# Last output tile in column parts of 384 and 128, the last 128 columns stored by two queues of 64 token rows each

## The chip, the cores and the metric

The kernel runs on one core of one Trainium2 chip. The metric is the device time of one execution, in microseconds (us). I quote medians over several executions. The trace's own span, from the first to the last recorded instruction, is about 1.7 us shorter than that time (178.7 against 180.4 us in the profiled run of the kernel before). PE is the tensor engine, ACT the scalar engine and DVE the vector engine; SP only issues transfers here. A transfer (DMA) is issued on the queue of SP or ACT, its packets then move the bytes, and I say that it has landed when the last of its 16 landing records is in.

## The reference

Two branches read the same 2048 tokens of 512 values, and a gate mixes them:

```python
x = A_x
g = sigmoid((x * gate_w).sum(-1, keepdims=True))
a = linear_attention(x, A_wqkv) @ A_wo        # 32 heads of 16
b = (silu(x @ B_w1) * (x @ B_w3)) @ B_w2      # F = 1376
return g * a + (1 - g) * b                    # 1 x 2048 x 512, bfloat16
```

## The kernel before

Tokens go through in four blocks of 512, each with four output tiles of 128 token rows. An output tile sums, in one PSUM tile, 4 matmuls of the attention branch, 1 of the FFN remainder and 10 of the FFN. It is then scaled per token and stored. Only the sixteenth tile, with which the kernel ends, is cut by columns:

```python
# loads, all on the SP queue
w2_r = B_w2[0:FM, :].rearrange("(fc f) d -> f fc d", f=P)
for fcs in (slice(0, FC // 2), slice(FC // 2, FC)):
    dq.dma_start(out=w2_sb[:, fcs, :], in_=w2_r[:, fcs, :])
# ... (cut)
def emit_out(tb, tt):
    # ... (cut)
    if t < NT - 1:
        parts = [(0, D, True)]
    else:
        h, q3 = D // 2, 3 * D // 4
        parts = [(0, h, True), (h, q3, False), (q3, D, True)]
    o_out = work.tile([P, D], BF16, tag="o_out", name="o_out")
    lo = 0
    for i, (a, b, store) in enumerate(parts):
        o_ps = psX.tile([P, b - a], FP32, tag=f"XP{2 + (tt + i) % 2}", name="o_ps")
        # ... 4 + 1 + 10 matmuls of b - a columns into o_ps (cut)
        if i < 2:
            nc.scalar.activation(out=o_out[:, a:b], in_=o_ps[:], func=ACT.Copy,
                                 scale=omg[:, t : t + 1])
        else:
            nc.vector.tensor_scalar(out=o_out[:, a:b], in0=o_ps[:],
                                    scalar1=omg[:, t : t + 1], scalar2=None, op0=ALU.mult)
        if store:
            rows = out_pairs[t // 2, t % 2] if t < TPB else out2d[t * P : (t + 1) * P, :]
            nc.sync.dma_start(out=rows[:, lo:b], in_=o_out[:, lo:b])
            lo = b
```

Of the kernel before, what the change touches and what calls it, by code (L numbers as in the profile page):

```python
# [9 lines left out]
ALU = mybir.AluOpType  # L10
# [7 lines left out]
def kernel(  # L18
# [12 lines left out]
    nc = tc.nc  # L31
    P = nc.NUM_PARTITIONS

    Bb, S, D = A_x.shape
# [4 lines left out]
    NT = S // P  # L39
    TB = 512  # L40
    NTB = S // TB
    TPB = TB // P
    FC = F // P
    FR = F - FC * P
    FM = FC * P
# [4 lines left out]
    out2d = out.flatten_outer_dims()  # L50
# [21 lines left out]
    w2_sb = consts.tile([P, FC, D], BF16, name="w2_sb")  # L72
# [7 lines left out]
    dq = nc.sync  # L80
    x_pairs = x2d[0:TB, :].rearrange("(g p j) d -> g p j d", p=P, j=2)
    out_pairs = out2d[0:TB, :].rearrange("(g p j) d -> g j p d", p=P, j=2)
# [6 lines left out]
    for tb in range(1, NTB):  # L89
        dq.dma_start(  # L90
            out=xT[:, :, tb * TB : (tb + 1) * TB], in_=x2d[tb * TB : (tb + 1) * TB, :],
# [3 lines left out]
            out=x_sb[:, tb * TPB : (tb + 1) * TPB, :], in_=x_r[:, tb * TPB : (tb + 1) * TPB, :]  # L95
# [4 lines left out]
    with nc.allow_non_contiguous_dma(reason="one gate weight per partition and chunk"):  # L100
        dq.dma_start(
            out=wr_sb[:, :, 2 * FR : NR], in_=gate_w.rearrange("(kc d o) -> d kc o", d=P, o=1)
# [3 lines left out]
        dq.dma_start(out=w1_sb[:, :, fsl], in_=w1_r[:, :, fsl])  # L106
        dq.dma_start(out=w3_sb[:, :, fsl], in_=w3_r[:, :, fsl])
    dq.dma_start(out=wo_sb[:], in_=A_wo.rearrange("(kc d) n -> d kc n", d=P))
    w2_r = B_w2[0:FM, :].rearrange("(fc f) d -> f fc d", f=P)
    for fcs in (slice(0, FC // 2), slice(FC // 2, FC)):  # L110
        dq.dma_start(out=w2_sb[:, fcs, :], in_=w2_r[:, fcs, :])
    dq.dma_start(out=w2r_sb[:FR, :], in_=B_w2[FM:F, :])

    pk_sb = consts.tile([P, NT, D], BF16, name="pk_sb")
# [5 lines left out]
        out=bm, in_=bm, pattern=[[-Dh, HPC], [0, Dh]], compare_op=ALU.is_ge, fill=0.0,  # L120
# [3 lines left out]
        out=bm, in_=bm, pattern=[[Dh, HPC], [0, Dh]], compare_op=ALU.is_ge, fill=0.0,  # L124
# [6 lines left out]
    omg = consts.tile([P, NT], FP32, name="omg")  # L131
# [200 lines left out]
    def emit_out(tb, tt):  # L332
        t = tb * TPB + tt
        tsl = slice(tt * P, (tt + 1) * P)

        if t < NT - 1:
            parts = [(0, D, True)]
        else:
            h, q3 = D // 2, 3 * D // 4
            parts = [(0, h, True), (h, q3, False), (q3, D, True)]  # L340
        o_out = work.tile([P, D], BF16, tag="o_out", name="o_out")
        lo = 0
        for i, (a, b, store) in enumerate(parts):
            o_ps = psX.tile([P, b - a], FP32, tag=f"XP{2 + (tt + i) % 2}", name="o_ps")
            for c in range(KC):
                nc.tensor.matmul(  # L346
                    o_ps[:], lhsT=st[tb, "pqT"][:, c, tsl], rhs=W_sb[:, c, a:b],
                    start=(c == 0), stop=False,
                )
            nc.tensor.matmul(  # L350
                o_ps[:], lhsT=st[tb, "hTr"][:FR, tsl], rhs=w2r_sb[:FR, a:b],
                start=False, stop=False,
            )
            for fc in range(FC):
                nc.tensor.matmul(  # L355
                    o_ps[:], lhsT=st[tb, "hT"][:, fc, tsl], rhs=w2_sb[:, fc, a:b],
                    start=False, stop=(fc == FC - 1),
                )
            if i < 2:
                nc.scalar.activation(  # L360
                    out=o_out[:, a:b], in_=o_ps[:], func=ACT.Copy, scale=omg[:, t : t + 1]
                )
            else:
                nc.vector.tensor_scalar(  # L364
                    out=o_out[:, a:b], in0=o_ps[:], scalar1=omg[:, t : t + 1], scalar2=None,
                    op0=ALU.mult,
                )
            if store:
                rows = out_pairs[t // 2, t % 2] if t < TPB else out2d[t * P : (t + 1) * P, :]
                nc.sync.dma_start(out=rows[:, lo:b], in_=o_out[:, lo:b])  # L370
                lo = b


    k0 = [psM.tile([P, D], FP32, tag="mm", name=f"k0_{t}") for t in range(TPB)]
# [33 lines left out]
    for c in range(KC):  # L408
# [7 lines left out]
        out=kvT_sb[:], in0=kvT_ps[:],  # L416
# [26 lines left out]
    for tb in range(NTB):  # L443
        for fc in range(FC if tb == 0 else 0, FC):
            emit_ffn(tb, fc)
        nx = tb + 1
        for tt in range(TPB):
            if nx < NTB:
                emit_q(nx, tt, psX, "XP0")
                if tt % 2 == 0:  # L450
                    emit_rem(nx, tt // 2, psX, "XP1")
            emit_out(tb, tt)
            if nx < NTB:
                emit_den(nx, tt)
        if nx < NTB:
            emit_norm(nx)
# [30 lines left out]
```

## Time and profile before

| what | kernel before |
|---|---|
| time, median of 6 executions | 180.28 us (180.18 to 180.48) |
| span of the profiled one | 178.7 us |
| tensor engine (PE) busy | 174.1 us, 97% |
| last tile on PE | 172.46 to 175.80 us |
| last scaling (DVE) | 175.88 to 176.23 us |
| last store issued | 176.30 us |

The page's first lines give each engine's busy time with its share and its number of instructions. The second part gives the clock granted to PE in tenths, over 40 slices:

```profile
span 178.7 us, 2472 instructions
...
PE 174.1 (97%) x877; PEld 84.6 (47%) x893; DVE 119.3 (67%) x205; ACT 66.6 (37%) x126; POOL 61.3 (34%) x69
...
PEclk9999999999999999999999999999999999999999
```

PE has work nearly all the time, at full clock. So the change can act only where PE's work ends and the last result has still to leave the chip. The chain that ended last, in the view from 169 us on (start, duration, what):

```profile
...
172.46 0.44 PE o_ps L346 x4
172.90 0.11 PE o_ps L350
173.01 1.09 PE o_ps L355 x10
174.10 0.22 PE o_ps L346 x4
174.33 0.06 PE o_ps L350
174.38 0.56 PE o_ps L355 x10
174.94 0.22 PE o_ps L346 x4
175.17 0.06 PE o_ps L350
175.23 0.57 PE o_ps L355 x10
...
175.88 0.35 DVE o_out L364
```

The three groups of 15 matmuls take 1.64, 0.84 and 0.85 us. What follows is in the timeline from 175.7 us on, and in the DMA issues from 176.3 us on (operation, KB, us from issue to landing):

```profile
176.30 0.33 SPq L370 DMA_DIRECT2D out_dram<-o_out  x1
```

```profile
out_dram<-o_out SPq DMA_DIRECT2D x1, 64.0 KB, 1.5
```

The issue keeps the SP queue busy for 0.33 us, and the data has landed 1.5 us after the issue began. The records of the single packets and landings are finer. Counted from the end of the last scaling, the first packet leaves at 0.90 us, the last landing is at 1.60 us, and the span ends at 2.45 us. I call that last figure the tail.

### The profile page before, as it was taken

The numbers are of one execution on the slowest core, as the hardware profiler recorded it, in microseconds if no ns is written. First come the engines' busy times: TensorE is split into PE (matmuls) and PEld (weight loads), VectorE is DVE, ScalarE is ACT, GpSimd is POOL, SyncE is SP. The second block draws the span as 40 slices with busy tenths as digits, with TensorE's granted clock in tenths as the row PEclk, the third lists the DMA queues.
The fourth block names the chain that finished last, engine by engine and source line by source line (L and its number), as shares of the span: only waits on it lengthen the run. The fifth ranks groups of instructions, "written<-read, shape, count | busy, mean of one in ns | idle before, by whom it ended". The sixth has DMA issues, their size and how long they took to land.

```text
span 178.7 us, 2472 instructions
## 1 busy us (share of the span) xinstructions
PE 174.1 (97%) x877; PEld 84.6 (47%) x893; DVE 119.3 (67%) x205; ACT 66.6 (37%) x126; POOL 61.3 (34%) x69
## 2 busy tenths in 40 slices
PE   8999999999999999999999999999999999999993
PEld 4444444474444545444454544444545444444463
DVE  1588867997998837398786375978754669776000
ACT  3642323476533333342433333342433323341221
POOL 5187575736353323262003232620032328100000
PEclk9999999999999999999999999999999999999999
DMA  5999999901005010124000111240001023300011
GB/s 178 263 272 245 267 321 369 321 6 28 9 12 107 0 48 29 44 55 92 0 4 6 38 37 37 59 93 2 0 7 59 14 62 64 61 0 0 29 44 50
DMA packets 29085, 14.88 MB, mean 83 GB/s; under 512 B 19632, under 2 KB 28816, under 8 KB 29072
## 3 DMA queue, kind: packets, MB, share of 16 engines
q1 hardware_dynamic: 28800, 14.46, 30.2%
q10 hardware_dynamic: 272, 0.26, 0.5%
q8 instruction: 7, 0.11, 0.3%
q14 instruction: 6, 0.05, 0.1%
HBM read 8.42 MB, written 2.10 MB: 59 GB/s over the span
## 4 chain that ended last, share of the span: by engine, by line
PE 97%; issue 1%; DVE 0%; DVEq 0%
PE o_ps L355 19%; PE gate_ps L310 19%; PE up_ps L318 19%; PE o_ps L346 8%; PE q_ps L217 8%; PE XP L204 8%; PE k_ps L184 6%; PE r_ps L241 3%; PE k L184 2%; PE o_ps L350 2%; PE warm L161 2%; PE xTp L174 1%; PE kvT_ps L411 1%; PE W_ps L438 0%; DVE o_out L364 0%
## 5 line engine op out<-in xcount | busy, mean ns | idle before, releaser
L310 PE MATMUL gate_ps<-xT,w_sb 128*128 128x512 bf16 x156 | 40.7, 379 | 0.2
L318 PE MATMUL up_ps<-xT,w_sb 128*128 128x512 bf16 x156 | 40.5, 379 | 0.2
L225 POOL TENSOR_TENSOR qz<-pq,z_sb 128x512 f32<-128x512 bf16 x16 | 18.5, 1165 | 60.3 <-DVE pq L145 58.4
L323 ACT ACTIVATE th<-gate_ps 128x512 bf16<-128x512 f32 x40 | 23.9, 597 | 38.1 <-PE gate_ps L310 36.6
L355 PE MATMUL o_ps<-w_sb,hT 128*128 128x512 bf16 (+2 forms) x176 | 37.3, 354 | 0.2
L325 DVE SCALAR_TENSOR_TENSOR gs<-th,gate_ps 128x512 bf16<-128x512 bf16 x40 | 27.3, 684 | 5.8 <-ACT th L323 5.3
L328 DVE TENSOR_TENSOR hT<-up_ps,gs 128x512 bf16<-128x512 f32 x40 | 27.6, 691 | 3.8
L142 DVE TENSOR_SCALAR phi_m<-phi_e 128x512 bf16<-128x512 bf16 x32 | 15.2, 475 | 18.9 <-ACT phi_e L140 18.8
L355 PEld LDWEIGHTS <-hT 128*128 128x128 bf16 x180 | 16.8, 97 | 17.9
L318 PEld LDWEIGHTS <-w_sb 128*128 128x128 bf16 x160 | 15.6, 98 | 18.9
L310 PEld LDWEIGHTS <-w_sb 128*128 128x128 bf16 x160 | 15.6, 98 | 18.7
L360 ACT ACTIVATE o_out<-o_ps,omg 128x512 bf16<-128x512 f32 (+2 forms) x17 | 11.2, 656 | 30.4 <-PE o_ps L355 30.4
L290 POOL TENSOR_TENSOR pqn<-pq,rden 128x512 bf16<-128x512 bf16 x16 | 16.6, 1057 | 14.0 <-DVE rden L283 11.7
L194 POOL TENSOR_TENSOR pks<-pks,pk_sb 128x512 f32<-128x512 f32 x15 | 17.3, 1155 | 8.1 <-DVE pk_sb L145 7.5
L228 DVE TENSOR_REDUCE den<-qz 128x32 f32<-128x512 f32 x16 | 11.0, 684 | 9.0 <-POOL qz L225 8.9
L346 PE MATMUL o_ps<-W_sb,pqT 128*128 128x512 bf16 (+2 forms) x71 | 16.5, 355 | 0.1
L217 PE MATMUL q_ps<-wq_sb,xT 128*128 128x512 bf16 x63 | 16.4, 379 | 0.1
L204 PE MATMUL XP<-pk_sb,x_sb 128*128 128x512 bf16 x62 | 16.0, 379 | 0.1
L140 ACT ACTIVATE phi_e<-k_ps 128x512 bf16<-128x512 f32 x12 | 7.2, 597 | 14.4 <-PE k_ps L184 12.2
L140 ACT ACTIVATE phi_e<-q_ps 128x512 bf16<-128x512 f32 x16 | 9.6, 597 | 7.8 <-PE q_ps L217 6.7
L184 PE MATMUL k_ps<-wk_sb,xT 128*128 128x512 bf16 x48 | 12.3, 379 | 0.1
L145 DVE SCALAR_TENSOR_TENSOR pq<-q_ps,phi_m 128x512 bf16<-128x512 f32 x16 | 11.1, 691 | 0.5
(59 smaller groups left out, 119.5 us busy)
## 6 DMA issues: line engine op xcount, KB each, us to landing
w_sb<-in_B_w_dram SPq DMA_DIRECT2D x6, 640.0 KB, 8.5
out_dram<-o_out SPq DMA_DIRECT2D x15, 128.0 KB, 1.7
x_sb<-in_A_x_dram SPq DMA_DIRECT2D x3, 512.0 KB, 4.4
x_sb<-in_A_x_dram SPq DMA_DIRECT2D x2, 256.0 KB, 3.5
wq_sb<-in_A_wqkv_dram SPq DMA_DIRECT2D x1, 512.0 KB, 6.6
wv_sb<-in_A_wqkv_dram SPq DMA_DIRECT2D x1, 512.0 KB, 6.5
wo_sb<-in_A_wo_dram SPq DMA_DIRECT2D x1, 512.0 KB, 9.5
wk_sb<-in_A_wqkv_dram ACTq DMA_DIRECT2D x1, 256.0 KB, 3.7
```

Of the source, the lines that this page charges most:

```text
L184: nc.tensor.matmul(k_ps[:], lhsT=xT[:, kc, t * P : (t + 1) * P], rhs=wk_sb[:, kc, :], start=(kc == 0), stop=(kc == KC - 1),)
L194: nc.gpsimd.tensor_add(pks[:], pks[:], pk_sb[:, t, :])
L204: nc.tensor.matmul(XP_ps[dc][:], lhsT=x_sb[:, t, dc * P : (dc + 1) * P], rhs=pk_sb[:, t, :], start=(t == 0), stop=(t == NT - 1),)
L217: nc.tensor.matmul(q_ps[:], lhsT=xT[:, kc, ts_tok], rhs=wq_sb[:, kc, :], start=(kc == 0), stop=(kc == KC - 1),)
L225: nc.gpsimd.tensor_tensor(out=qz[:], in0=st[tb, "pq"][:, tt, :], in1=z_sb[:], op=ALU.mult)
L310: nc.tensor.matmul(gate_ps[:], lhsT=w1_sb[:, kc, fsl], rhs=xT[:, kc, tok_sl], start=(kc == 0), stop=(kc == KC - 1),)
L318: nc.tensor.matmul(up_ps[:], lhsT=w3_sb[:, kc, fsl], rhs=xT[:, kc, tok_sl], start=(kc == 0), stop=(kc == KC - 1),)
L323: nc.scalar.activation(out=th[:], in_=gate_ps[:], func=ACT.Tanh, scale=0.5)
L325: nc.vector.scalar_tensor_tensor(out=gs[:], in0=th[:], scalar=1.0, in1=gate_ps[:], op0=ALU.add, op1=ALU.mult)
L328: nc.vector.tensor_tensor(out=st[tb, "hT"][:, fc, :], in0=up_ps[:], in1=gs[:], op=ALU.mult)
L346: nc.tensor.matmul(o_ps[:], lhsT=st[tb, "pqT"][:, c, tsl], rhs=W_sb[:, c, a:b], start=(c == 0), stop=False,)
L355: nc.tensor.matmul(o_ps[:], lhsT=st[tb, "hT"][:, fc, tsl], rhs=w2_sb[:, fc, a:b], start=False, stop=(fc == FC - 1),)
```

## The change

The intent: fewer matmuls at the end (two groups instead of three), a last store half as large, and that store shared by two queues, so that it is out sooner. Of the loads, two become one; they are issued from 24.5 us on.

```diff
-    w2_r = B_w2[0:FM, :].rearrange("(fc f) d -> f fc d", f=P)
-    for fcs in (slice(0, FC // 2), slice(FC // 2, FC)):
-        dq.dma_start(out=w2_sb[:, fcs, :], in_=w2_r[:, fcs, :])
+    dq.dma_start(out=w2_sb[:], in_=B_w2[0:FM, :].rearrange("(fc f) d -> f fc d", f=P))
@@ emit_out
-        if t < NT - 1:
-            parts = [(0, D, True)]
-        else:
-            h, q3 = D // 2, 3 * D // 4
-            parts = [(0, h, True), (h, q3, False), (q3, D, True)]
+        parts = [(0, D)] if t < NT - 1 else [(0, 3 * D // 4), (3 * D // 4, D)]
@@
-            if i < 2:
+            if i == 0:
                 nc.scalar.activation(
                     out=o_out[:, a:b], in_=o_ps[:], func=ACT.Copy, scale=omg[:, t : t + 1]
                 )
-            else:
-                nc.vector.tensor_scalar(
-                    out=o_out[:, a:b], in0=o_ps[:], scalar1=omg[:, t : t + 1], scalar2=None,
-                    op0=ALU.mult,
-                )
-            if store:
-                rows = out_pairs[t // 2, t % 2] if t < TPB else out2d[t * P : (t + 1) * P, :]
-                nc.sync.dma_start(out=rows[:, lo:b], in_=o_out[:, lo:b])
-                lo = b
+                nc.sync.dma_start(out=rows[:, a:b], in_=o_out[:, a:b])
+                continue
+            nc.vector.tensor_scalar(
+                out=o_out[:, a:b], in0=o_ps[:], scalar1=omg[:, t : t + 1], scalar2=None,
+                op0=ALU.mult,
+            )
+            for q, ps in ((nc.scalar, slice(0, P // 2)), (nc.sync, slice(P // 2, P))):
+                q.dma_start(out=rows[ps, a:b], in_=o_out[ps, a:b])
```

(Left out here: the line that sets `rows` moved ahead of the loop, and the loop lost `store` and `lo`.)

More of the change, by code (lines that the diff above doesn't have):

```diff
@@ L334, in emit_out @@
         tsl = slice(tt * P, (tt + 1) * P)
-        if t < NT - 1:
-            parts = [(0, D, True)]
-        else:
-            h, q3 = D // 2, 3 * D // 4
-            parts = [(0, h, True), (h, q3, False), (q3, D, True)]
+        parts = [(0, D)] if t < NT - 1 else [(0, 3 * D // 4), (3 * D // 4, D)]
         o_out = work.tile([P, D], BF16, tag="o_out", name="o_out")
-        lo = 0
-        for i, (a, b, store) in enumerate(parts):
+        rows = out_pairs[t // 2, t % 2] if t < TPB else out2d[t * P : (t + 1) * P, :]
+        for i, (a, b) in enumerate(parts):
             o_ps = psX.tile([P, b - a], FP32, tag=f"XP{2 + (tt + i) % 2}", name="o_ps")
```

## The prediction

> **What bounds the kernel now.** The tensor engine. The page gives a span of 178.7 us with PE busy 97%; the chain of waits that ended last is 97% PE, and the granted clock is 1.00 throughout. The change can only touch the end. There the chain runs: the last tile's three matmul groups from 172.46 to 175.80 us, the DVE scaling of the last 128 columns (0.35 us, from 175.88), the store's issue on the SP queue at 176.30 (0.33 us), its packets from about 177.15 to 177.45, its landing at about 177.8, the end at 178.7.
>
> **What the change does.**
>
> 1. Matmuls. Three groups of 15 (256, 128, 128 columns) become two (384, 128), so 15 matmuls and 15 weight loads go. The chain shows 1.64 us for 15 of 256 (109 ns each), 0.84 to 0.85 us for 15 of 128 (56 ns each), 3.24 us for 15 of 512 (216 ns each); between them I estimate 162 ns for 384 columns, 2.43 us for the group. Then 2.43 + 0.85 = 3.28 us against 3.34: PE ends 0.06 us sooner, all of it on the chain.
> 2. Evictions. ACT does 384 columns (an estimate of 0.58 us, between 0.47 for 256 and 0.69 for 512) and is done before the last group ends. The 128-column DVE scaling stays 0.35 us.
> 3. Stores. The 384-column store is issued near 175.6, well before the last issue near 176.24. The last store carries 32 KB instead of 64 KB, in rows of 256 B instead of 512 B, over two queues. The packet records show 25 to 27 ns for 512 B and 44 to 48 ns for 1024 B; the last store's 128 packets took only 0.3 us in all. The rest is fixed: 0.86 us from issue to first packet, 0.3 us from last packet to landing, 0.9 us from there to the end. The Trainium skill, "DMA: Bandwidth & Descriptors", says in "Anatomy of one DMA" that the fixed part is mostly the write receipt and does not scale with size; this trace agrees roughly (128 KB land in 1.7 us, 64 KB in 1.5). The same page ("Specifications") says transfers under 512 B need a read-modify-write; nothing in this trace shows such a store, so the narrow rows may give the gain back. I estimate 0 to -0.1 us from size, and 0 to +0.1 from the narrow rows and the ACT queue's issue (0.45 us at the start, beside 0.39 on SP).
> 4. The second FFN weight is loaded in one transfer instead of two. Both were issued by 28.4 us and their first reader runs near 57 us: nothing on the chain.
>
> **Sum.** -0.06 (PE), about -0.04 (store): -0.1 us. I predict 180.15 us, range 179.85 to 180.45. Faster by over 2%: 0.01; within 2%: 0.98; slower by over 2%: 0.01.
>
> **What would show it.** In the chain: the 384 group near 2.43 us and 128 group near 0.85; last matmul to end 0.06 us sooner; DVE still 0.35 us; no ACT or SP wait before the last issue. In DMA issues: two 16 KB stores, each 1.3 to 1.6 us to landing.
>
> **What would make it wrong.** A slow ACT issue, or two simultaneous issues that serialize (the last landing later by 0.2 to 0.4 us); narrow writes with a slow receipt (the same size); a shift of instruction fetch that stalls PE elsewhere; or a late wait for the merged weight. None reaches 2% (3.6 us).

## The result, and the profile after

The changed kernel took 180.99 us in the median (180.63 to 181.35, 6 executions), beside 180.28 us before. The ratio is 1.0037, with a 95% interval of 1.0021 to 1.0053. The kernel became slightly slower: well inside 2%, but clear of noise, and 0.54 us above the top of the predicted range.

The chain in the changed kernel, in the view from 169 us on:

```profile
...
172.93 0.65 PE o_ps L340 x4
173.58 0.16 PE o_ps L344
173.74 1.63 PE o_ps L349 x10
175.37 0.22 PE o_ps L340 x4
175.59 0.06 PE o_ps L344
175.65 0.57 PE o_ps L349 x10
...
176.31 0.35 DVE o_out L359
```

PE now needs 2.44 + 0.85 = 3.29 us for the last tile, where it needed 3.34: the gain of 0.05 us is there. The last lines of the timeline from 175 us on, and the DMA issues from 174.9 us on:

```profile
176.06 0.33 SPq L357 DMA_DIRECT2D out_dram<-o_out  x1
176.31 0.35 DVE L359 TENSOR_SCALAR o_out<-o_ps,omg 128x128 bf16<-128x128 f32 x1 [11.82 <-PE o_ps L349]
176.69 0.56 SPq L364 DMA_DIRECT2D out_dram<-o_out  x1
176.69 0.55 ACTq L364 DMA_DIRECT2D out_dram<-o_out  x1
```

```profile
out_dram<-o_out SPq DMA_DIRECT2D x1, 96.0 KB, 1.6
out_dram<-o_out SPq DMA_DIRECT2D x1, 16.0 KB, 1.8
out_dram<-o_out ACTq DMA_DIRECT2D x1, 16.0 KB, 2.1
```

A quarter of the bytes per store, and yet each issue lasts 0.56 us instead of 0.33, and the landings come 1.8 and 2.1 us after it instead of 1.5. The tail grew from 2.45 to 2.98 us.

The spans of the two profiles differ by 0.96 us, and this is where, by the trace's records:

| stretch | before | changed | difference |
|---|---|---|---|
| start, to the 33rd weight load of PE | 6.82 | 7.28 | +0.46 |
| middle, from the 33rd to the 801st weight load | 154.89 | 154.90 | +0.01 |
| from there to PE's end | 14.08 | 14.03 | -0.05 |
| PE's end to the end of the last scaling | 0.45 | 0.45 | 0.00 |
| tail | 2.45 | 2.98 | +0.53 |

I take the start to be chance and not the change's doing: the programs are the same there, and the start differed in all profiles. The chain of the first 7 us, the kernel before first, then the changed one:

```profile
0.84 3.04 PE warm L161 x9
3.88 0.85 PE xTp L174 x8
```

```profile
0.80 3.27 DMA x_sb<-in_A_x_dram
4.07 0.04 issue
4.11 1.03 PE xTp L172 x8
```

In the changed kernel's profile the first load of x landed at 4.07 us, after the warm-up matmuls had ended, and PE waited for it. In the kernel before it landed at 3.63 us, in time. Over the fifteen profiles that landing lies between 3.45 and 4.37 us, and the start between 6.43 and 7.28 us. That landing alone does not set the start: in h_stagger (below) it came at 3.63 us and the start was still 7.25, in j_half_only it came at 4.37 and the start was 6.92. All three landings after 4 us are in the changed kernel or variants of it (3 of 10 such profiles, against 0 of 5 of the kernel before and its variants), which is too few to tell from chance. The kernel before itself ran between 180.05 and 181.12 us over its rounds. The middle was 154.89 or 154.90 us in every one of the fifteen. So the tail is what has to be explained. It and PE's gain make +0.48 us. The medians differ by 0.71 us, but the interval of the ratio allows 0.38 to 0.96 us, so 0.48 agrees with it.

### The profile page after: what moved, and what is told of

It reads as the page before. It is cut to its first block, busy times and chain, and to the rows that moved or that the text cites. A ratio compares the mean times of both kernels' runs of the same rounds, so it can differ in the third digit from the quotient of the medians.

```text
span 179.6 us, 2458 instructions
## 1 busy us (share of the span) xinstructions
PE 175.1 (97%) x878; PEld 83.8 (47%) x878; DVE 119.3 (66%) x205; ACT 66.4 (37%) x125; POOL 61.3 (34%) x69
## 4 chain that ended last, share of the span: by engine, by line
PE 96%; DMA 2%; DVE 0%; issue 0%; DVEq 0%
PE o_ps L349 19%; PE up_ps L316 19%; PE gate_ps L308 19%; PE o_ps L340 8%; PE q_ps L215 8%; PE XP L202 8%; PE k_ps L182 6%; PE r_ps L239 3%; PE k L182 2%; PE o_ps L344 2%; DMA x_sb<-in_A_x_dram 2%; PE xTp L172 1%; PE kvT_ps L404 0%; PE W_ps L431 0%; DVE o_out L359 0%; PE z_ps L422 0%
## 5 line engine op out<-in xcount | busy, mean ns | idle before, releaser
L316 PE MATMUL up_ps<-xT,w_sb 128*128 128x512 bf16 x160 | 41.1, 379 | 0.0
L349 PEld LDWEIGHTS <-hT 128*128 128x128 bf16 x170 | 16.2, 97 | 18.5
L354 ACT ACTIVATE o_out<-o_ps,omg 128x512 bf16<-128x512 f32 (+1 forms) x16 | 10.9, 681 | 30.9 <-PE o_ps L349 30.9
```

Source lines behind the costliest of these rows:

```text
L316: nc.tensor.matmul(up_ps[:], lhsT=w3_sb[:, kc, fsl], rhs=xT[:, kc, tok_sl], start=(kc == 0), stop=(kc == KC - 1),)
L349: nc.tensor.matmul(o_ps[:], lhsT=st[tb, "hT"][:, fc, tsl], rhs=w2_sb[:, fc, a:b], start=False, stop=(fc == FC - 1),)
```

## The experiments

The theories. T: two queues that issue at the same moment slow each other, and their packets go one after the other. R: rows of 256 B are written slowly. Q: the ACT queue is slow. W: the single weight load, or something that it moves, costs time. T fell in the second round, and U came in its place: a store of 64 rows is itself slow to issue. Two more rivals, N and V, are stated in the expectations of the runs that test them. All numbers in us; "last landing" and "tail" count from the end of the last scaling.

| run | last store or stores | issue | last landing | tail | median | ratio (95%) |
|---|---|---|---|---|---|---|
| before | 128 rows x 512 B, SP | 0.33 | 1.60 | 2.45 | 180.28 | |
| changed | 64 x 256 B on SP, 64 on ACT | 0.56, 0.55 | 2.09 | 2.98 | 180.99 | 1.0037 (1.0021 to 1.0053) |
| a_one_store | 128 x 256 B, SP | 0.33 | 1.48 | 2.57 | 180.42 | 0.9995 (0.9978 to 1.0011) |
| e_one_store_act | 128 x 256 B, ACT | 0.36 | 1.51 | 2.40 | 180.37 | 0.9994 (0.9979 to 1.0009) |
| b_w2_split | as changed | 0.56, 0.56 | 2.08 | 2.91 | 181.12 | 1.0032 (1.0013 to 1.0052) |
| c_before_two_queues | 64 x 512 B on SP, 64 on ACT | 0.56, 0.53 | 2.36 | 3.19 | 181.03 | 1.0035 (1.0022 to 1.0048) |
| d_both_on_sp | 64 x 256 B twice, SP | 0.56, 0.58 | 2.45 | 3.48 | 181.12 | 1.0047 (1.0032 to 1.0063) |
| h_stagger | as changed, ACT 0.39 earlier | 0.53, 0.56 | 2.61 | 3.44 | 181.75 | 1.0081 (1.0066 to 1.0095) |
| i_four_stores | 32 x 256 B, two on each | 0.32 to 0.41 | 2.70 | 3.64 | 181.59 | 1.0071 (1.0054 to 1.0088) |
| j_half_only | 64 x 256 B, SP, other half not written | 0.56 | 1.80 | 2.88 | 180.95 | 1.0031 (1.0017 to 1.0045) |
| m_cols_at_once | 128 x 128 B on SP, 128 on ACT | 0.33, 0.38 | 1.61 | 2.52 | 180.29 | 0.9992 (0.9972 to 1.0012) |
| n_rows_96_32 | 96 x 256 B on SP, 32 on ACT | 0.34, 0.38 | 1.64 | 2.54 | 180.51 | 0.9997 (0.9978 to 1.0016) |
| l_cols_two_queues | 128 x 256 B on SP, on ACT 0.88 earlier | 0.33, 0.36 | 1.48 | 2.42 | 180.34 | 1.0002 (0.9985 to 1.0020) |
| f_before_w2_one | as before | 0.33 | 1.60 | 2.50 | 180.13 | 0.9999 (0.9982 to 1.0016) |

The kernel before ran anew in each round, with medians of 180.34 to 180.46 us beside the experiments. So compare the ratios, not the medians.

### First round: which part of the change

**a_one_store.** The changed kernel with a single last store.

```diff
-            for q, ps in ((nc.scalar, slice(0, P // 2)), (nc.sync, slice(P // 2, P))):
-                q.dma_start(out=rows[ps, a:b], in_=o_out[ps, a:b])
+            nc.sync.dma_start(out=rows[:, a:b], in_=o_out[:, a:b])
```

> The changed kernel, but its last 128 columns go out in one 128-row store on the SP queue (still 256 B rows, still the single weight load). The measure is the tail: from the end of the last DVE scaling to the end of the span, 2.45 us in the kernel before and 2.97 us in the changed one. Theory T (two issues at the same moment slow each other and their packets go one after the other): issue back to 0.33 us, tail 2.4 to 2.5 us, median 180.2 to 180.3 if the start is undisturbed. Rival R (rows of 256 B are written slowly): tail stays at 2.9 to 3.0 us. Rival W (the single weight load, or what else moved, makes the kernel slower): median stays near 180.9 whatever the tail does.

The slowdown is gone (0.9995). The issue is 0.33 us again, and with rows of 256 B the last landing is even 0.12 us sooner than before. R and W fall. The timeline and the DMA issue of this run:

```profile
176.40 0.33 SPq L363 DMA_DIRECT2D out_dram<-o_out  x1
```

```profile
out_dram<-o_out SPq DMA_DIRECT2D x1, 32.0 KB, 1.4
```

The tail, 2.57 us, is a little longer than I had expected, although the landing was early. From the landing to the end it took 1.09 us here instead of 0.85, because ACT reached the last barrier late. The same is seen (1.03 and 1.08 us) in the two other runs in which ACT has nothing after its 384-column scaling, and in no other. Why is open.

**b_w2_split.** The changed kernel with the weight load in two halves again.

```diff
-    dq.dma_start(out=w2_sb[:], in_=B_w2[0:FM, :].rearrange("(fc f) d -> f fc d", f=P))
+    w2_r = B_w2[0:FM, :].rearrange("(fc f) d -> f fc d", f=P)
+    for fcs in (slice(0, FC // 2), slice(FC // 2, FC)):
+        dq.dma_start(out=w2_sb[:, fcs, :], in_=w2_r[:, fcs, :])
```

> The changed kernel with the second FFN weight loaded in two halves again; both last stores stay. T: tail stays 2.9 to 3.0 us, median 180.6 to 181.0, the same as the changed kernel. W: median back to 180.3. T says nothing of the 0.45 us by which the first matmul group started later in the changed kernel's profile (first x load landed at 4.07 us instead of 3.63); if the weight load had to do with that, the first x load lands before 3.7 us here, and the median is about 0.3 us below the changed kernel's.

The tail stays long (2.91 us) and the kernel stays slow (181.12 us). This profile's first load of x landed at 3.65 us and its own time was only 180.53 us, but of its five other executions four took 181.0 us or more. The early landing is what the expectation named for a load that causes the slow start; the median, which should then have fallen by 0.3 us, did not fall. So nothing points to the load as the cause of the slow start.

**c_before_two_queues.** The kernel before with nothing but its last store cut into two 64-row halves.

```diff
+                if i < 2:
                     nc.sync.dma_start(out=rows[:, lo:b], in_=o_out[:, lo:b])
+                else:
+                    for q, ps in ((nc.scalar, slice(0, P // 2)), (nc.sync, slice(P // 2, P))):
+                        q.dma_start(out=rows[ps, lo:b], in_=o_out[ps, lo:b])
```

> The kernel before, with its last store (256 columns, 512 B rows) cut into two 64-row halves on the ACT and SP queues, nothing else. T: both issues take about 0.55 us instead of 0.33, tail 2.9 to 3.05 us, median 0.4 to 0.6 us above the kernel before. R: issues may slow but tail stays 2.4 to 2.5 us and the median equals the kernel before. W: the same as the kernel before.

This alone makes the kernel before as slow as the changed one (1.0035 beside 1.0037). Cutting the last store into two halves of rows is the cause; whether by the rows or by the second queue, this run can't tell. ACT began its issue 0.30 us after SP here and still needed 0.53 us for it; I can't say what delayed it. The timeline and the DMA issues:

```profile
176.15 0.56 SPq L374 DMA_DIRECT2D out_dram<-o_out  x1
176.45 0.53 ACTq L374 DMA_DIRECT2D out_dram<-o_out  x1
```

```profile
out_dram<-o_out SPq DMA_DIRECT2D x1, 32.0 KB, 2.1
out_dram<-o_out ACTq DMA_DIRECT2D x1, 32.0 KB, 2.0
```

The tail of 3.19 us lies above T's range. One landing record of each half came late, 2.18 us where the 15 others were in by 1.94, and 2.36 where they were in by 2.21; h_stagger, below, shows the same.

**e_one_store_act.** As a_one_store, but the store is issued on ACT.

```diff
-            for q, ps in ((nc.scalar, slice(0, P // 2)), (nc.sync, slice(P // 2, P))):
-                q.dma_start(out=rows[ps, a:b], in_=o_out[ps, a:b])
+            nc.scalar.dma_start(out=rows[:, a:b], in_=o_out[:, a:b])
```

> As the one-store kernel, but that one store is issued on the ACT queue. T: what costs is that two are issued at once, so one alone on ACT is like one on SP: issue 0.33 to 0.4 us, tail 2.4 to 2.6 us. Rival Q (the ACT queue itself is slow to start at the end of the kernel): tail 2.9 us or more.

The issue took 0.36 us, the landing was at 1.51 us, and the tail of 2.40 us is the shortest of all. Q falls. At this point nearly every result agreed with T (the tails of a_one_store and c_before_two_queues lay 0.07 and 0.14 us above its ranges).

### Second round: is it the two queues at once?

**d_both_on_sp.** Both 64-row halves on SP, one after the other.

```diff
-            for q, ps in ((nc.scalar, slice(0, P // 2)), (nc.sync, slice(P // 2, P))):
+            for q, ps in ((nc.sync, slice(0, P // 2)), (nc.sync, slice(P // 2, P))):
```

> The changed kernel with both 64-row halves of the last store on the SP queue, one issue after the other. The measure is the time from the end of the last scaling to the last landing: 1.60 us in the kernel before, 2.09 in the changed one, 1.48 with one store on SP. T (what costs is that both queues issue at the same moment): each issue back to 0.33 us or less, the second starts about 0.38 us after the first, the last landing at 1.75 to 1.9 us, that is later than one store but sooner than two queues, and the median 180.45 to 180.75. Rival N (two transfers cost the same extra on any queue, by their number or their small size): last landing at 2.05 us or later.

T failed here. With nothing else being issued, the halves took 0.56 and 0.58 us, and the last landing was at 2.45 us, later than with two queues. That fits the rival N, which falls only in the fourth round. The timeline (two issues in one line) and the DMA issues from 174.9 us on:

```profile
175.97 1.19 SPq L364 DMA_DIRECT2D out_dram<-o_out  x2
```

```profile
out_dram<-o_out SPq DMA_DIRECT2D x2, 16.0 KB, 1.8
```

**h_stagger.** The scaling in two halves of rows on DVE, so that the issues hardly overlap.

```diff
-            nc.vector.tensor_scalar(
-                out=o_out[:, a:b], in0=o_ps[:], scalar1=omg[:, t : t + 1], scalar2=None,
-                op0=ALU.mult,
-            )
             for q, ps in ((nc.scalar, slice(0, P // 2)), (nc.sync, slice(P // 2, P))):
+                nc.vector.tensor_scalar(
+                    out=o_out[ps, a:b], in0=o_ps[ps, :], scalar1=omg[ps, t : t + 1],
+                    scalar2=None, op0=ALU.mult,
+                )
                 q.dma_start(out=rows[ps, a:b], in_=o_out[ps, a:b])
```

> The changed kernel with the last scaling cut into rows 0 to 63 and rows 64 to 127, one after the other on DVE, so that the ACT queue issues its half while DVE still works on the SP queue's half and the two issues hardly overlap. T: each issue 0.33 to 0.40 us, the last landing 1.45 to 1.6 us after the end of the last scaling (which itself ends about 0.35 us later than before). N: last landing still 1.8 to 2.1 us after the end of the last scaling. The median says little, about 180.5 to 180.8 either way.

T missed again: 0.53 us on ACT, although the SP issue came only 0.39 us after it began, and 0.56 us on SP. ACT's half landed 1.76 us after its issue began. Of the SP half's 16 landing records 15 are in by 1.82 us and the last is at 2.61 us; an instruction fetch, one packet of 8 KB, ran from 1.24 to 1.81 us, and the last packets of this half began as it ended, at 1.81 us, where the others had begun by 1.44. So the fetch most likely held up one DMA engine; no run was made to test that. Apart from it, neither half was later than a 64-row store by itself (j_half_only): the first packets left 1.19 and 1.21 us after the issues began.

**i_four_stores.** Four stores of 32 rows, two on each queue.

```diff
-            for q, ps in ((nc.scalar, slice(0, P // 2)), (nc.sync, slice(P // 2, P))):
+            for r in range(4):
+                q, ps = (nc.scalar, nc.sync)[r % 2], slice(r * P // 4, (r + 1) * P // 4)
                 q.dma_start(out=rows[ps, a:b], in_=o_out[ps, a:b])
```

> The changed kernel with the last 128 columns in four stores of 32 rows, two on each queue: the suspected cost doubled, the bytes the same. T: four issues of about 0.55 us, two after two; last landing 2.6 to 2.75 us after the end of the scaling, median 181.3 to 181.7. If the cost lay in the bytes or rows moved and not in the issues, last landing stays at 2.1 us.

The last landing, 2.70 us, lay in the expected range, but not for the expected reason. The issues of 32 rows took 0.34 and 0.37 us for the first pair, at the same moment on two queues, which T forbids, and this pair landed by 1.41 and 1.57 us. The second pair began 0.4 and 0.7 us after the end of the scaling. 15 of 16 landings were in by 1.85 and 2.09 us, and a single late one made each 2.53 and 2.70. Again an 8 KB instruction fetch ran just then, from 1.38 to 1.84 us, and the last packets of the two began at 1.84 and 1.87. So that the landing met T's range is luck. The shape matters, and 64 rows stand out.

**f_before_w2_one.** The kernel before with the weight in one load.

```diff
-    w2_r = B_w2[0:FM, :].rearrange("(fc f) d -> f fc d", f=P)
-    for fcs in (slice(0, FC // 2), slice(FC // 2, FC)):
-        dq.dma_start(out=w2_sb[:, fcs, :], in_=w2_r[:, fcs, :])
+    dq.dma_start(out=w2_sb[:], in_=B_w2[0:FM, :].rearrange("(fc f) d -> f fc d", f=P))
```

> The kernel before with the second FFN weight in one load, nothing else changed. All theories that survive say the same as the kernel before: median within 0.2 us of it; the middle of the kernel (33rd to 801st weight load of the tensor engine, 154.89 us in every profile so far) unchanged to 0.02 us. W: slower by 0.2 us or more, the rest of the changed kernel's median that its tail does not explain.

No effect: the ratio is 0.9999 and the middle is 154.89 us. W is closed.

### Third round: 64 rows by themselves

**k_sweep.** The kernel before, earlier output tiles stored in pieces; one look.

```diff
-                nc.sync.dma_start(out=rows[:, lo:b], in_=o_out[:, lo:b])
+                cuts = {4: (64, 64), 5: (32, 32, 32, 32), 6: (96, 32), 7: (112, 16), 8: (64, 64),
+                        9: (48, 80), 10: (16, 16, 16, 16, 64), 11: (32, 64, 32), 13: (96, 32)}
+                r = 0
+                for n in cuts.get(t, (P,)):
+                    q = nc.scalar if t == 8 else nc.sync
+                    q.dma_start(out=rows[r : r + n, lo:b], in_=o_out[r : r + n, lo:b])
+                    r += n
```

> The kernel before, with output tiles 4 to 13 stored in pieces of 16 to 112 rows (each 1 KB wide), on SP, and on ACT for tile 8; tile 12 and the last ones whole. Only issue durations and landings are read. Theory T fell, for a 64-row store took 0.56 us to issue on one queue alone. Theory U (a store of 64 rows takes about 0.23 us longer to issue than one of 128 or of 32, whatever the queue and width): 64-row pieces 0.53 to 0.58 us in every tile, 32- and 128-row pieces 0.32 to 0.41. Rival V (it is the change of shape from the issue before it that costs): the first piece of any new row count is long, the second of the same count short.

All six 64-row pieces took 0.51 to 0.60 us to issue, on SP and on ACT (0.53 and 0.60), first or second in a row: V falls, and U's range of 0.53 to 0.58 was a little narrow. The other counts, where no transpose and no 64-row piece was issued just before, took 0.31 to 0.42 us: 16, 32, 48, 80, 96 and 112 rows. There are exceptions. One 32-row piece after a 96-row one took 0.55, one 16-row piece 1.12, and a store that directly follows a transpose (by about 0.1 us) takes 0.50 to 0.53 with 16, 96 or 128 rows too, in the kernel before as well (once 1.15). Stores that came 2.7 and 12.9 us after a transpose took 0.32 and 0.36. 32-row pieces issued just after 64-row ones took 0.52 and 0.58. So this run alone would not show that it is the count of 64; the stores at the end of the other runs, which follow no transpose, do. Time from the end of the issue to the landing was 1.45 to 1.50 us for five of the six 64-row pieces (1.32 for the other), about 1.36 for 128 rows and about 1.15 for 32. Three pieces of this run in short windows of its timeline, the issues of 64 rows (the second of tile 4; the first directly follows a transpose), of 32 (tile 5) and of 112 (tile 7):

```profile
100.05 0.57 SPq L375 DMA_DIRECT2D out_dram<-o_out  x1
...
102.26 0.34 SPq L375 DMA_DIRECT2D out_dram<-o_out  x1
...
111.20 0.32 SPq L375 DMA_DIRECT2D out_dram<-o_out  x1
```

**j_half_only.** Only the SP half is stored; the result is wrong.

```diff
-            for q, ps in ((nc.scalar, slice(0, P // 2)), (nc.sync, slice(P // 2, P))):
+            for q, ps in ((nc.sync, slice(P // 2, P)),):
```

> The changed kernel with only the SP half of the last store; the other 64 rows of the last 128 columns are never written, so the result is wrong there on purpose. U: issue 0.56 us, last landing 1.8 us after the end of the scaling (as the SP half of the changed kernel), so the row count alone gives 0.2 to 0.33 us of the 0.48, and the rest belongs to the second queue. If the second queue also slowed the SP half: landing at 1.5 to 1.6 us and issue 0.33.

U is right to the digit: 0.56 us, landing at 1.80 us. A single store of 16 KB lands 0.32 us later than the single store of 32 KB in a_one_store, and its first packet leaves at 1.23 us instead of 0.86. Half the work, done later. The landing gives only +0.20 us over the kernel before, yet the tail grew by 0.43 and the ratio (1.0031) is nearly the changed kernel's: the remaining 0.23 us lie between the landing and the end, where ACT is late as in a_one_store (1.07 us instead of 0.84). So the ratio of this run is not the cost of the 64 rows alone. The timeline and the DMA issue:

```profile
176.32 0.56 SPq L364 DMA_DIRECT2D out_dram<-o_out  x1
```

```profile
out_dram<-o_out SPq DMA_DIRECT2D x1, 16.0 KB, 1.8
```

**l_cols_two_queues.** The kernel before, its last store cut by columns.

```diff
+                if i < 2:
                     nc.sync.dma_start(out=rows[:, lo:b], in_=o_out[:, lo:b])
+                else:
+                    m = (lo + b) // 2
+                    for q, cs in ((nc.scalar, slice(lo, m)), (nc.sync, slice(m, b))):
+                        q.dma_start(out=rows[:, cs], in_=o_out[:, cs])
```

> The kernel before, its last store (256 columns) cut by columns and not by rows: 128 rows of 128 columns on ACT and on SP at the same moment. It separates two queues at once from 64 rows. U plus a cost of the second queue: issues 0.33 and 0.36 us (no 64-row cost), SP half lands at 1.5 to 1.6 us, ACT half about 0.3 us later, at 1.75 to 1.95; median 0.15 to 0.4 us above the kernel before. If two queues at once cost nothing with 128 rows: both land by 1.6 us and the median equals the kernel before. If what remained of T is right for any shape (issues slow each other): issues 0.55 us.

This did not test what it should. The ACT half needed only the part that ACT had scaled, so it was issued 0.88 us ahead of the other. The kernel came out as before (1.0002). It shows only that two queues with 128 rows, not at once, cost nothing.

### Fourth round: what the second queue adds

**m_cols_at_once.** The changed kernel, the last 128 columns in two halves of 64 columns and all rows, both after the one scaling.

```diff
-            for q, ps in ((nc.scalar, slice(0, P // 2)), (nc.sync, slice(P // 2, P))):
-                q.dma_start(out=rows[ps, a:b], in_=o_out[ps, a:b])
+            m = (a + b) // 2
+            for q, cs in ((nc.scalar, slice(a, m)), (nc.sync, slice(m, b))):
+                q.dma_start(out=rows[:, cs], in_=o_out[:, cs])
```

> The changed kernel, its last 128 columns cut into two halves of 64 columns with all 128 rows, issued on ACT and SP at the same moment after the one scaling. If the second queue waits for the first one's stream in any shape: issues 0.33 and 0.36 us, SP half lands at about 1.5 us after the scaling and the ACT half 0.2 to 0.3 us later, 1.7 to 1.8; median 0.1 to 0.35 us above the kernel before. If the second queue costs only with 64 rows: both land by 1.55 us and the median is that of the one-store kernel, 180.2 to 180.4.

The halves landed at 1.45 (SP) and 1.61 us (ACT). The timeline:

```profile
175.99 0.33 SPq L365 DMA_DIRECT2D out_dram<-o_out  x1
176.00 0.38 ACTq L365 DMA_DIRECT2D out_dram<-o_out  x1
```

The result lies between the two expectations: the second queue adds 0.16 us, not 0.2 to 0.3, and the ratio, 0.9992, shows no loss. N falls: two small transfers at once are not slow as such.

**n_rows_96_32.** The changed kernel with the rows cut at 32.

```diff
-            for q, ps in ((nc.scalar, slice(0, P // 2)), (nc.sync, slice(P // 2, P))):
+            for q, ps in ((nc.scalar, slice(0, P // 4)), (nc.sync, slice(P // 4, P))):
```

> The changed kernel with its row cut at 32 instead of 64: rows 0 to 31 on ACT and 32 to 127 on SP, at the same moment. U (it is the count of 64): issues 0.32 to 0.4 us each, last landing 1.5 to 1.75 us after the scaling, median within 0.3 us of the kernel before, and clearly under the changed kernel. If any row cut over two queues costs the same: last landing at 2.0 us or later, median near 180.9.

This is the deciding run: the same bytes, the same two queues, the same moment, and only the row counts are others. The ratio is 0.9997, where the changed kernel had 1.0037, and the intervals do not overlap. Issues, landing (1.64 us) and median are as U expected. The packets of the two stores ran side by side here, 0.87 to 1.13 us (SP) and 0.96 to 1.16 (ACT). The timeline and the DMA issues:

```profile
176.23 0.34 SPq L364 DMA_DIRECT2D out_dram<-o_out  x1
176.24 0.38 ACTq L364 DMA_DIRECT2D out_dram<-o_out  x1
```

```profile
out_dram<-o_out SPq DMA_DIRECT2D x1, 24.0 KB, 1.5
out_dram<-o_out ACTq DMA_DIRECT2D x1, 8.0 KB, 1.6
```

## Why the prediction was wrong

- **PE (point 1): right.** Predicted 2.43 + 0.85 us and 0.06 us saved; measured 2.44 + 0.85 and 0.05.
- **Scalings (point 2): right.** ACT's 384 columns took 0.58 us, as estimated, and DVE's 128 stayed at 0.35.
- **The weight load (point 4): right.** b_w2_split and f_before_w2_one show no effect.
- **Stores (point 3): this step failed.** The text summed "0 to -0.1 us from size, and 0 to +0.1 from the narrow rows and the ACT queue's issue", about -0.04 us together, and took 0.86 us from issue to first packet as fixed. That interval is not fixed: it depends on the row count. Measured, the tail grew by 0.53 us. The last landing after the scaling went from 1.60 to 2.09 us, +0.48 before rounding, and the two stores landed 1.8 and 2.1 us after their issue, not 1.3 to 1.6. Of this the 64-row half makes +0.20 (j_half_only: 1.80), because its issue takes 0.56 us instead of 0.33 and its first packet leaves 1.20 us after the issue begins instead of 0.84. The other half makes the remaining +0.29: its packets began at 1.51 us, 1.47 after its issue began, when the first half's had ended at 1.46. With other row counts the second queue adds 0.16 us (m_cols_at_once, n_rows_96_32), and 128 rows on one queue land at 1.48. The narrow rows, which I had feared, show no cost: 1.48 against 1.60 us with half the bytes, and 15 to 18 ns for a packet of 256 B where one of 512 B took 25 to 27. Nor is ACT slow (1.51).
- **What would make it wrong.** The text named "two simultaneous issues that serialize (the last landing later by 0.2 to 0.4 us)". This was half of it. The packets of the two halves did follow one another, and the second half landed 0.28 us after the first; when the two issues were 0.39 us apart (h_stagger), neither waited. But the issues did not serialize: a 64-row issue takes 0.56 us with one queue alone, and that part was not foreseen. With other row counts the two queues cost the kernel nothing that can be measured. T, fitted to the whole 0.48, passed nearly all of the first round.
- **The range** (179.85 to 180.45) was also narrow for another reason. The three executions of the kernel before that were known then lay within 0.16 us, but over the later rounds it ran between 180.05 and 181.12, and the start varied by up to 0.85 us between profiles.

Open: why 64 rows are slow to issue and 32 or 96 are not; why the second of two simultaneous 64-row stores starts its packets 0.27 us later than one alone, where the two runs with other row counts show at most 0.06 beside e_one_store_act; why ACT comes late to the last barrier in three runs; and whether the 0.2 us of the changed kernel's median that the tail doesn't explain is only chance in the start, as I take it to be.

Of the kernels tried, e_one_store_act has the shortest tail, 0.05 us under the kernel before, beside PE's 0.05 us. In time it can't be told from the kernel before (0.9994, 0.9979 to 1.0009).

## What to carry to other kernels

The store at the very end of this kernel was paid mostly in issue time and delay, not in bytes: half of the bytes saved 0.12 us of 1.60 to the landing. Cutting the last store of 64 or 32 KB into pieces brought nothing here, and a cut into 64 rows cost more (0.5 us) than was saved elsewhere (0.05 us). Before giving part of a DMA to a second queue, look in the trace at how long the issue of exactly that shape lasts, and change one dimension at a time; "two queues" and "64 rows" came in one edit here, and the first four experiments could not tell them apart. For effects below 1% split the span into start, middle and tail: the middle here repeats to 0.01 us, while the start moved by 0.85 us and the time from the last landing to the end by 0.26.

## What the Trainium skill lacked or had wrong

- "DMA: Bandwidth & Descriptors", section "Why a DMA increments its semaphore by 16 and not by 1", says that the number of DMA engines follows from the largest divisor up to 16 of the row counts, so 64, 96 and 128 rows should all use 16. The landing records agree (16 for each), but no page that I found says that a 64-row DMA needs 0.51 to 0.60 us to issue, on SP and ACT, where 128 rows need 0.33 (when no transpose came directly before) and the other counts from 16 to 112 rows mostly 0.31 to 0.42.
- The same page, "Rules for kernel authors", says that spreading DMAs over the queues "only saves sequencer issue time". For two 64-row halves that holds against the same two on SP (last landing 2.09 against 2.45 us), but against one whole store it saves nothing: two issues of 0.56 us beside one of 0.33. This is no gap in the page: the same table advises against two transfers to disjoint partition halves, because they serialize. For 64 and 64 rows issued at once the runs agree (packets from 1.51 us on after others until 1.46); for 96 and 32 rows the packets ran side by side and nothing was lost (0.9997), which the page does not tell.
- The same page, "Anatomy of one DMA", has the fixed part at about 2.0 us, as independent of the size and mostly the write receipt. It says this of DMAs issued by the gpsimd engine; the prediction used it for SP and ACT. Here small stores landed 1.4 to 1.5 us (128 rows), 1.8 us (64 rows) after the issue began, so it changed with the number of rows. And the larger part came before the first packet (0.84 us in the kernel before), not after the last one (0.36 us to the last landing).
- The same page, "Specifications", has transfers under 512 B do a read-modify-write. No cost of it shows for 128 rows of 256 B into HBM: landing at 1.48 us, against 1.60 for 512 B rows with twice the bytes. The same bytes in both widths were not compared.
- No page that I found mentions that a plain store of 128 rows that directly follows a DMA transpose on the same queue (by 0.09 us) is issued in 0.53 us (once 1.15), and the next in 0.33 to 0.35.
